# Two layers of sliding attention and SiLU feed-forward on one core: the planner's durations and DMA rings, and three moved steps

## The chip, the cores and the metric

The kernel runs on one core of a Trainium2 chip. The metric is its device time in microseconds (us). The core has five engines with a queue each, which run their instructions in order: TensorE (PE, matmuls; PEld is its weight load), VectorE (DVE), ScalarE (ACT), GpSimd (POOL) and SyncE (SP, which here only issues DMAs). An instruction starts when it is at the head of its queue and the semaphores that it waits for are there.

## The reference

The input has 2048 rows of 576 values. Two layers, each of two steps, with the same weights in both:

```python
x = x + _A_ref(_layernorm(x, axis=-1), A_wqkv, A_wo)
x = x + _B_ref(_layernorm(x, axis=-1), B_w1, B_w2)
```

`_A_ref` is attention with 32 heads of 18 values, where each row looks at 8 rows: itself and those 2, 4, ... 14 rows before it. `_B_ref` is a feed-forward: 576 to 4608 values, SiLU, and back to 576. All values are float32.

## The kernel before, in words

**Numbers.** Matmuls run in float16 with two halves for each operand: a high half and what is left of it. Three products (high by high, high by low, low by high) stand for one (`passes`). The scale of each weight is a power of two, found on the chip from the sum of its squares.

**Chunks and stages.** The rows are cut into four chunks of 512, each with four tiles of 128 rows (index `j`). A stage `s` from 0 to 7 is one chunk in one layer (`s = 4 * layer + chunk`). For each stage the work is: attention (`attention`, VectorE for the most part), its projection back into `x` (`project`), a layer norm, and a feed-forward (`ffn` for stages 0 to 2, `ffn_pairs` with fewer products for stages 3 to 7). "Chunk 1" and "second chunk" both mean stage 1. The q, k and v of chunks 1, 2 and 3 of the first layer are made early by `qkv_ahead`, while VectorE works on attention 0, and go through DRAM. Stage 0's feed-forward also splits the weights: raw tiles come by POOL's DMAs (L851 to L855), ScalarE sums their squares (L872, L874), PE adds them up over the partitions (L881, L882), ScalarE makes the high halves (L891, L896) and VectorE the low ones (L893, L898), and POOL stores them for the later stages. `prepare` then makes, for stages 3 to 7, the weights that `ffn_pairs` reads (`wfs`).

**Turning a tile.** `transposed` (L426) brings a tile of 128 rows with its 9 blocks of 128 columns into the form that PE needs. Either PE turns the nine blocks into PSUM (L435) and ScalarE copies them out (L437), or SP issues one DMA transpose (L439). `project` turns the attention tile `yh` into `yo` in the first way for stage 0, and by DMA for all others. Its matmuls are L817, 28 for each tile. The PSUM tiles `acc` (two, of two banks each) serve L435, L817 and the feed-forward's second product (L1157, L1096). Its first product is L1138 (`z`) or, in the pairs, L1042.

**Layer norm.** `layer_norm` has ways to get mean and variance: VectorE's `bn_stats` and `bn_aggr` (L481, L482), or, with `on_act == 2`, two passes of ScalarE with a sum (`total`: a copy, and a square of what is left when the mean is taken off), with VectorE's `mean` between them. The four norms that stand ahead of attention 0 use the first way.

**Scales of the feed-forward's middle.** `group_scale` (L907) makes, for a group of weights, a table of scales `sh` and its inverse `d2`, with four small VectorE instructions. After stage 0 it is called for four groups of nine weights (stages 1 and 2) and for four groups of 10, 8, 10 and 8 (the pairs).

**What sets the order.** The order of all instructions is made by a planner written into the kernel (`Plan`, L59). Each operation has an engine, a duration written into the code by hand, a priority (lower goes first), what it reads and writes, and `nbytes` if it is a DMA. `order` (L112) plays the program through: whenever an engine is free, the ready operation of the lowest priority whose buffers are free goes next. A DMA takes its issue time, then 1.2 us, its bytes at 0.33 MB per us (shared among the queues that have one under way), and 0.9 us; another engine sees an end 0.2 us later. The instructions are then written out in that order, each engine's queue in its own, and the chip runs them so whatever times come true. On the chip, DMAs of POOL on one hand, and those of SP and ACT on the other, take turns over eight semaphores; the order of `before` is made without them.

Of the kernel before, what the change touches and what calls it, by code (L numbers as in the profile page):

```python
# [16 lines left out]
P = 128  # L17
D = 576
# [36 lines left out]
class Op:  # L55
    __slots__ = ("eng", "dur", "fn", "prio", "seq", "deps", "outs", "n", "bufs", "nbytes", "start", "end", "table")


class Plan:  # L59
# [18 lines left out]
    def op(self, eng, dur, fn, reads=(), writes=(), prio=0.0, nbytes=0, table=None, after=()):  # L78
        o = Op()
        o.eng, o.dur, o.fn, o.prio, o.seq, o.nbytes, o.table = eng, dur, fn, prio, len(self.ops), nbytes, table  # L80
        o.outs, o.end = [], None
# [30 lines left out]
    def order(self):  # L112
# [10 lines left out]
        taken = {}  # L123

# [58 lines left out]
        while done < len(self.ops):  # L183
# [14 lines left out]
            for e in engines:  # L198
# [7 lines left out]
                while ready[e]:  # L206
                    x = heapq.heappop(ready[e])
                    need = [b for b in x[2].bufs if b.slot is None]
                    n = {}
                    for b in need:  # L210
                        n[b.tag] = n.get(b.tag, 0) + 1
                    if all(len(open_slots(t)) - want.get(t, 0) >= c for t, c in n.items()) and all(
                            self.turns[b.tag] in (None, b.turn) for b in need):
                        o = x[2]
                        break
                    for t, c in n.items():
                        want[t] = want.get(t, 0) + c
                    back.append(x)
# [22 lines left out]
                if o.nbytes:  # L241
                    queues[e].append([now + dur + self.DMA_IN, o.nbytes / self.DMA_RATE, o])
# [10 lines left out]
def sliding_attention_silu_ffn(ctx: ExitStack, tc: tile.TileContext, x, wqkv, wo, w1, w2, out):  # L253
# [143 lines left out]
    cg = cp.tile([P, NFT // G0], F32, name="cg")  # L397
    su = cp.tile([P, NU + 1], F32, name="su")
# [27 lines left out]
    def transposed(src, dst, key, j, prio, on_pe=False):  # L426


        if on_pe:
# [6 lines left out]
            op("PE", 0.8, turn, [(src, 0), (src, 1)], [m], prio)  # L436
            return op("ACT", 1.05, lambda: nc.scalar.activation(  # L437
                dst(), fl(T(m).bitcast(F16))[:, 0:9 * P].rearrange("p (a b) -> p a b", a=9), AF.Copy), [m], [(key, j)], prio - 9)
        return op("SP", 1.7, lambda: nc.sync.dma_start_transpose(dst(), fl(T(src))), [(src, 0), (src, 1)], [(key, j)], prio,  # L439
# [27 lines left out]
    def layer_norm(xs, prio, into, on_act, on_pe=False, late=[]):  # L467
# [18 lines left out]
        if on_act == 2:  # L486
            for j in range(NJ):
                op("ACT", 0.95, lambda j=j: total(j, 0), [xs[j]], [(st, j)], prio)
            op("DVE", 0.2, mean, [(st, j) for j in range(NJ)], [(nt, 0)], prio)
            for j in range(NJ):  # L490
                op("ACT", 0.95, lambda j=j: total(j, 1), [xs[j], (nt, 0)], [(st, j)], prio)
        else:
            for j in range(NJ):
                op("DVE", 1.15, lambda j=j: stats(j), [xs[j]], [(st, j), (mv, j)], prio)

        op("DVE", 2.4, lambda: newton(st, mv, nt, on_act, LNS), [(st, j) for j in range(NJ)] + [(mv, j) for j in range(NJ) if on_act != 2], [nt], prio)
        for j in range(NJ):
# [12 lines left out]
            if on_act in (1, 2) or on_act == 3 and j % 2 == 0:  # L510
                op("ACT", 0.74, lambda j=j, y=y: nc.scalar.activation(T(y), T(xs[j]), AF.Identity,
                                                                      bias=T(nt)[:, 2, j:j + 1]),
                   [xs[j], nt], [y, (xT, "hold")], prio)
                op("ACT", 0.74, lambda j=j, y=y, yh=yh: nc.scalar.activation(
                    fl(T(yh))[:, 0:D], T(y), AF.Copy, scale=T(nt)[:, 1, j:j + 1]), [y, nt], [(yh, 0)], prio)
                o = op("DVE", 0.95, lambda j=j, y=y, yh=yh: halves_lo(T(y), fl(T(yh)), T(nt)[:, 1, j:j + 1]),
                       [y, nt, (yh, 0)], [(yh, 1)], prio)
            else:
                op("DVE", 0.6, norm, [xs[j], (mv, j), nt] + late, [y, (xT, "hold")], prio)
                o = op("DVE", 1.2, halves, [y], [(yh, 0), (yh, 1)], prio)  # L520
# [20 lines left out]
    def raw_wq(u):  # L541
# [4 lines left out]
        for k in range(5):  # L546
# [8 lines left out]
            op("SP" if u else "ACT", 0.8 if k < 4 else 1.3, load, [], [rs[k]], WQ[u] if u else -20, nbytes=P * 3 * UC * 4, after=gate[3:4] if u > 1 else ())  # L555
            op("ACT", 0.8, square, [rs[k]], [("accq", u, k)], WQ[u])
# [10 lines left out]
        op("PE", 0.3, total, [("accq", u, k) for k in range(5)], [m], WQ[u])  # L567
        op("DVE", 0.9, scale, [m], [("su", u)], WQ[u])
        for k in range(5):
# [5 lines left out]
            op("ACT", 0.65, hi, [rs[k], ("su", u)], [w.keys[k]], WQ[u])  # L575
            op("DVE", 0.65, lo, [rs[k], ("su", u), w.keys[k]], [w.keys[5 + k]], WQ[u])
# [3 lines left out]
    def store_wq(u, w, m):  # L580
# [7 lines left out]
        op("POOL", 2.8 if w.kind == "h" else 0.6, store, w.keys, [("wqs", u)], -0.6, nbytes=P * 20 * QR, after=marks[m:m + 1])  # L588
# [10 lines left out]
    def raw_wo():  # L599
        rs = [Buf("w2") for _ in range(5)]  # L600
        p = -1.02
        for k in range(5):
# [9 lines left out]
            op("POOL", 0.6 if k < 4 else 1.2, load, [], [rs[k]], p, nbytes=P * D * 5,  # L612
               after=marks[PACE_WO[k]:PACE_WO[k] + 1])
            op("ACT", 0.9, square, [rs[k]], [("acco", k)], p)
# [10 lines left out]
        op("PE", 0.3, lambda: nc.tensor.matmul(T(m)[:, :5], ones, acco, start=True, stop=True),  # L625
           [("acco", k) for k in range(5)], [m], p)
        op("DVE", 1.6, scale, [m] + [("su", u) for u in range(NU)], ["so"], p)
        for k in range(5):
# [6 lines left out]
            op("ACT", 0.8, hi, [rs[k], "so"], [(WO, k)], p)  # L635
            op("DVE", 0.8, lo, [rs[k], "so", (WO, k)], [(WO, 5 + k)], p)
# [16 lines left out]
    def qkv_ahead(c, u, xT, w):  # L653
# [3 lines left out]
        for j in range(NJ):  # L657
            m, g = Buf("z"), Buf("w1" if c < 3 else "hs")
            op("PE", 2.6, lambda j=j, m=m: qkv_matmul(xT, w, j, m), [(xT, j)] + w.keys, [m], p)
            op("ACT", 0.65, lambda m=m, g=g: nc.scalar.activation(stage(g), T(m)[:, :QR], AF.Copy,  # L660
# [5 lines left out]
            op("SP", 0.9, store, [g], [("qd", c, u)], p, nbytes=P * QR * 4)  # L666

    def no_keys():
# [7 lines left out]
        op("POOL", 2.2, fn, [g], [("qd0", u) for u in range(NU)], -20, nbytes=50000)  # L676

    def attention(s, xT, wq, more=None):
# [4 lines left out]
        for u in range(NU):  # L683
            kv, qt = Buf("kv"), Buf("qt")
            own = [(kv, j) for j in range(NJ)]
            if wq is None:
                def fetch(kv=kv, qt=qt, u=u):
# [5 lines left out]
                op("SP" if s == 1 else "POOL", 1.2, fetch, [("qd", c, u), ("qd0", u) if blk == 0 else ("eds", lay, par, u)],  # L693
                   own + [(qt, j) for j in range(NJ)] + [(kv, "halo"), (kv, "edge")], pr_, nbytes=P * 4 * UC * 26)
            else:
                w = wq(u)
                if blk == 0:
# [3 lines left out]
                    op("POOL", 1.6, clear, [], [(kv, "edge")], pr_)  # L701
                else:
# [5 lines left out]
                    op("SP", 0.8, edge, [("eds", lay, par, u)], [(kv, "edge")], pr_, nbytes=20000)  # L708
                for j in range(NJ):
# [7 lines left out]
                    op("PE", 2.7 if s else 2.9, lambda j=j, m=m, w=w: qkv_matmul(xT, w, j, m),  # L717
                       [(xT, j)] + w.keys, [m, (kv, "hold")] if lay else [m], pr_)
                    op("ACT", 0.9, evac, [m, ("su", u)], [(kv, j), (qt, j)], pr_ - (0 if s else 9))
# [7 lines left out]
                op(*(("POOL", 2.6) if lay else ("ACT", 3.2)), halo, own, [(kv, "halo")], pr_ - 0.2, nbytes=P * 14 * UC * 4)  # L727
                if blk == 0:
# [7 lines left out]
                    op("POOL", 0.6, save, own, [("eds", lay, par, u)], pr_, nbytes=20000)  # L736
# [4 lines left out]
            for j in range(0, NJ, 2):  # L741
# [9 lines left out]
                op("DVE", 2.57, mul, keys + [(qt, j), (qt, j + 1)], [pr], pr_)  # L751
                op("DVE", 2.57, red, [pr], [(lg, j)], pr_)
# [14 lines left out]
            op("DVE", 1.25 if blk == 0 else 0.9, soft_a, [], lgs + [mx], pr_)  # L767
            op("ACT", 0.45, lambda pe=pe, lg=lg: nc.scalar.activation(T(pe), T(lg), AF.Exp, scale=DH ** -0.5),
               lgs, [pe], pr_ - 0.2, table="exp")
            op("DVE", 1.1, soft_b, [], [pe, sm], pr_)  # L770
            for j in range(0, NJ, 2):
                pr = Buf("pr")

                for a in range(2):
# [5 lines left out]
                    op("DVE", 1.33, mul, keys + [pe], [(pr, a)], pr_)  # L780
# [6 lines left out]
                op("DVE", 2.63, tree, [], [(pr, 0), (pr, 1), (o, j, u), (o, j + 1, u)], pr_)  # L787
                if s == 0:
                    marks.append(op("POOL", 0.2, lambda j=j, u=u: nc.gpsimd.tensor_copy(
# [3 lines left out]
    def project(s, o, xs):  # L793

        pr_ = s - 1.0
        for j in range(NJ):
# [12 lines left out]
            op(*(("ACT", 0.74) if s < 2 else ("DVE", 0.5)), hi, src, [(oh, 0)], pr_)  # L809
            op("DVE", 0.95, lo, src + [(oh, 0)], [(oh, 1)], pr_)  # L810
            transposed(oh, lambda oT=oT: T(oT), oT, j, pr_, s == 0)
# [7 lines left out]
            op("PE", 3.5, mm, [(oT, j)] + [(WO, k) for k in range(10)], [acc], pr_)  # L819
# [453 lines left out]
```

## Time and profile before

| | us |
|---|---|
| median of three timed runs | 2188.64 (2187.58 to 2190.4) |
| the profiled execution, its own time | 2198.78 |
| its span, first to last instruction | 2197.0 |
| granted TensorE clock over the span | 0.993 of full speed |

A profile shows one execution. Its groups give a line of the kernel, an engine, an operation and its tiles (written <- read, buffer numbers left out), how many there are, the busy time, the mean of one in ns, and the engine's idle time just before them with what ended it. A timeline row gives start, duration, engine, line, operation, tiles, count, and in brackets the idle time before it. A table by stretch gives the length of the stretch, the busy time and count of PE, PEld, DVE, ACT and POOL, and then the granted clock, the busy share of the DMA engines and GB/s.

### The profile page before, as it was taken

What the parts mean: (1) busy time and instruction counts of PE and PEld (TensorE: products, weight loads), DVE (VectorE), ACT (ScalarE), POOL (GpSimd) and SP (SyncE); (2) the same over time, 40 slices, a digit from 0 to 9 for tenths busy, and PEclk for the clock granted to TensorE, in tenths of its full rate; (3) what the DMA queues carried; (4) which work ended last, traced back from release to release, by engine and by line L of the source; (5) the groups of instructions that cost most, each with busy time, mean ns of one, the idle gap of its engine ahead of it and who ended that gap; (6) DMA issues with size and microseconds to landing.
All of it is one profiled execution on the core that took longest, in us unless ns stands there. A gap on an engine that the chain in (4) does not pass through costs nothing.

```text
span 2197.0 us, 40182 instructions
## 1 busy us (share of the span) xinstructions
PE 2132.9 (97%) x15784; PEld 1541.9 (70%) x15784; DVE 1598.0 (73%) x2513; ACT 927.2 (42%) x1697; POOL 380.9 (17%) x639
## 2 busy tenths in 40 slices
PE   5999999899999999999999999999999999999999
PEld 3555556566666666686788777887688867888887
DVE  7898888799999985456985489756995569753222
ACT  6445576544334444342343344253342424333232
POOL 2124355343133443101100010000000000000000
PEclk9999999999999999999999999999999999999999
DMA  5577567777687676686657765496565955566443
GB/s 154 159 204 258 175 224 228 197 223 241 184 223 253 234 216 202 211 232 179 180 143 184 208 209 175 127 240 160 176 187 136 250 153 162 156 174 183 141 146 108
DMA packets 318741, 417.23 MB, mean 190 GB/s; under 512 B 141640, under 2 KB 242612, under 8 KB 312280
## 3 DMA queue, kind: packets, MB, share of 16 engines
q1 hardware_dynamic: 279568, 280.31, 45.6%
q0 software_dynamic: 35712, 129.17, 18.3%
q10 hardware_dynamic: 3272, 5.19, 0.9%
q8 instruction: 123, 2.02, 0.4%
q14 instruction: 66, 0.54, 0.1%
HBM read 298.47 MB, written 67.68 MB: 167 GB/s over the span
## 4 chain that ended last, share of the span: by engine, by line
PE 87%; DMA 6%; DVE 4%; ACT 1%; issue 1%; POOL 0%; SPq 0%; ACTq 0%; DVEq 0%; POOLq 0%
PE acc L1096 24%; PE acc L1157 13%; PE z L1138 13%; PE z L1042 10%; PE misc L1042 10%; PE z L647 7%; PE misc L647 5%; PE acc L817 5%; DMA w<-wfs 2%; DMA yo<-yh 1%; DMA w<-in_B_w_dram 1%; DVE pr L778 1%; DMA h<-in_A_wqkv_dram 1%; DVE pr L785 1%; DVE yh L422 0%
## 5 line engine op out<-in xcount | busy, mean ns | idle before, releaser
L1096 PE MATMUL acc<-w,h 128*128 128x288 f16 x4320 | 549.3, 286 | 0.6 <-DVE x L1105 0.6
L1096 PEld LDWEIGHTS <-h 128*128 128x128 f16 x4320 | 422.7, 98 | 106.5 <-issue 0.8
L1042 PEld LDWEIGHTS <-w 128*128 128x128 f16 x4410 | 431.8, 98 | 67.9 <-DMA w<-wfs 8.2
L1138 PE MATMUL z<-xb,w 128*128 128x512 f16 x1512 | 336.9, 383 | 11.5 <-ACT hs L1140 4.2
L1157 PE MATMUL acc<-w,h 128*128 128x288 f16 x2592 | 321.7, 286 | 0.0
L1157 PEld LDWEIGHTS <-h 128*128 128x128 f16 x2592 | 253.7, 98 | 65.8
L1042 PE MATMUL misc<-xb,w 128*128 128x256 f16 x2226 | 280.3, 273 | 3.9 <-DVE wq L1049 2.2
L1138 PEld LDWEIGHTS <-w 128*128 128x128 f16 x1512 | 148.8, 99 | 191.0 <-DVE w L893 7.5
L1042 PE MATMUL z<-xb,w 128*128 128x256 f16 x2184 | 276.2, 273 | 5.6 <-DMA w<-wfs 4.0
L824 DVE SCALAR_TENSOR_TENSOR x<-acc,d,x 128x576 f32<-128x576 f32 x135 | 109.7, 813 | 189.7 <-PE acc L1096 152.8
L647 PEld LDWEIGHTS <-xa 128*128 128x128 f16 x1344 | 132.1, 99 | 118.3 <-issue 8.4
L745 DVE TENSOR_TENSOR pr<-qt,kv 128x2304 f32<-128x2304 f32 x64 | 163.4, 2553 | 20.7 <-DMA kv<-kv 19.5
L778 DVE TENSOR_TENSOR pr<-kv,pe 128x1152 f32<-128x1152 f32 x128 | 169.6, 1352 | 1.0
L749 DVE TENSOR_REDUCE lg<-pr 128x128 f32<-128x2304 f32 x64 | 163.1, 2549 | 1.4
L1140 ACT ACTIVATE hs<-z,d 128x512 f32<-128x512 f32 x108 | 73.7, 682 | 165.8 <-PE z L1138 162.3
L785 DVE TENSOR_TENSOR pr<-pr 128x1152 f32<-128x1152 f32 (+1 forms) x128 | 135.1, 1056 | 3.2
L817 PE MATMUL acc<-wo,yo 128*128 128x288 f16 x896 | 117.4, 290 | 9.7 <-DMA yo<-yh 8.0
L1075 DVE SCALAR_TENSOR_TENSOR h<-wq,sh,h 128x1024 f16<-128x1024 f32 x60 | 76.8, 1280 | 65.0 <-ACT h L1072 65.0
L647 PE MATMUL z<-wq,xa 128*128 128x432 f16 x602 | 116.6, 349 | 2.7 <-ACT w L660 2.0
L647 PE MATMUL misc<-wq,xa 128*128 128x432 f16 x574 | 112.0, 350 | 3.4 <-ACT xa L437 2.5
L817 PEld LDWEIGHTS <-yo 128*128 128x128 f16 x896 | 88.7, 99 | 35.2 <-DMA yo<-yh 8.8
L1145 DVE SCALAR_TENSOR_TENSOR h<-hs,sh,h 128x512 f16<-128x512 f32 x108 | 79.5, 746 | 34.7 <-ACT h L1142 34.4
(186 smaller groups left out, 2297.3 us busy)
## 6 DMA issues: line engine op xcount, KB each, us to landing
w<-wfs SPq DMA_DIRECT2D x630, 160.0 KB
w<-w2s SPq DMA_DIRECT2D x252, 288.0 KB
w<-w1s SPq DMA_DIRECT2D x72, 320.0 KB
wfs<-xa POOLq DMA_DIRECT2D x18, 1120.0 KB, 5.5
wq<-wqs SPq DMA_DIRECT2D x17, 1080.0 KB
kv<-kd POOLq DMA_DIRECT2D x8, 1584.0 KB, 8.6
w1s<-w POOLq DMA_DIRECT2D x36, 320.0 KB, 4.2
w<-in_B_w_dram POOLq DMA_DIRECT2D x36, 288.0 KB, 4.0
```

Of the source, the lines that this page charges most:

```text
L647: nc.tensor.matmul(T(m)[:, :3 * UC], a, b, start=n == 0, stop=n == len(pl) - 1)
L745: nc.vector.tensor_tensor(T(pr), T(qt)[:, j:j + 2, None, :].to_broadcast([P, 2, W, UC]), win(T(kv), j, 2), op=ALU.mult)
L749: nc.vector.tensor_reduce(T(lg)[:, j:j + 2].rearrange("p a w h -> p (a w h)"), T(pr).rearrange("p a w (h d) -> p (a w h) d", d=DH), axis=A ...
L778: nc.vector.tensor_tensor(T(pr)[:, a].rearrange("p w (h d) -> p w h d", d=DH), v, T(pe)[:, j + a, :, :, None].to_broadcast([P, W, UH, DH]) ...
L785: nc.vector.tensor_tensor(t[:, :, 0:h, :], t[:, :, 0:h, :], t[:, :, h:2 * h, :], op=ALU.add)
L817: nc.tensor.matmul(T(acc)[:, h, 0:288], a, b[:, h * 288:(h + 1) * 288], start=n == 0, stop=n == len(pl) - 1)
L824: nc.vector.scalar_tensor_tensor(t, T(acc)[:, :, 0:288], d, t, op0=ALU.mult, op1=ALU.add)
L1042: nc.tensor.matmul(t, w[:, u, :], v[:, r, :], start=first and m == 0, stop=m == 6, skip_group_check=True)
L1096: nc.tensor.matmul(T(acc)[:, h, 0:288], T(hb[t])[:, a, f, j * P:(j + 1) * P], T(wbs[t][f])[:, w, h * 288:(h + 1) * 288], start=t == 0 and ...
L1138: nc.tensor.matmul(T(z), v, u, start=m == 0, stop=m == len(pl) - 1)
L1145: op("DVE", 0.75, lambda hs=hs, h=h, f=f: nc.vector.scalar_tensor_tensor(T(h)[:, 1, :], T(hs), shs[i][:, f:f + 1], T(h)[:, 0, :], op0=ALU. ...
L1157: nc.tensor.matmul(T(acc)[:, h, 0:288], T(hb[q])[:, a, j * P:(j + 1) * P], T(wbs[q][0])[:, w, h * 288:(h + 1) * 288], start=q == 0 and m = ...
```

## The change

Four things.

1. **Durations.** Some seventy of the planner's durations are new. Most are smaller by 0.03 to 0.25 us: 0.82 to 0.75 (L891), 0.9 to 0.81 (L893), 0.7 to 0.61 (L1140), 0.85 to 0.75 (L824), 2.57 to 2.49 (L745, L749), 1.33 to 1.28 (L778), 1.15 to 0.99 (L481), 0.8 to 0.5 (L435), 1.7 to 1.34 (L439), 0.5 to 0.38 (SP's loads of weights). PE's barely move: 3.05 to 3.02 (L1138), 0.74 to 0.737 (L1096, L1157), 0.78 to 0.763 (L1042), 2.6 to 2.56 (L647), 3.5 to 3.43 (L817). Some grow: 1.1 to 1.38 (the second half of the softmax), 1.25 to 1.42 and 0.9 to 0.98 (its first half), 2.4 to 2.55 (`newton`), 6.0 to 7.2 (`prepare`'s load), 1.7 to 1.83 (L851), 0.2 to 1.3 (L789, POOL's pace mark).
2. **Rings.** Each DMA operation has a number of `lanes`, the DMAs that it issues. The planner keeps a ring of the DMAs issued by POOL, and one by SP and ACT together. An operation may go only when those that would be eight places back have landed.
3. **Moved steps.** The attention tiles of stage 1 are turned by PE (`s < 2` for `s == 0`), and the norm of chunk 3 ahead of attention 0 takes its statistics on ScalarE (`2` for `True`).
4. **Tables.** `tables` takes the place of the eight calls of `group_scale` after stage 0.

```diff
+        rings = {"POOL": [], "SP": []}
+        rings["ACT"] = rings["SP"]
+
+        def landed(o):
+
+            if not o.nbytes:
+                return True
+            r = rings[o.eng][-8:]
+            return len(r) + o.lanes <= 8 or all(d.end is not None and d.end <= now for d in r[:len(r) + o.lanes - 8])
...
-                    if all(len(open_slots(t)) - want.get(t, 0) >= c for t, c in n.items()) and all(
+                    if landed(x[2]) and all(len(open_slots(t)) - want.get(t, 0) >= c for t, c in n.items()) and all(
...
                 if o.nbytes:
+                    rings[e].extend([o] * min(o.lanes, 8))
...
-        op("POOL", 6.0, load, ["wsc"], [w], prio, nbytes=P * 12 * P * 4)
+        op("POOL", 7.2, load, ["wsc"], [w], prio, nbytes=P * 12 * P * 4, lanes=8)
...
-            transposed(oh, lambda oT=oT: T(oT), oT, j, pr_, s == 0)
+            transposed(oh, lambda oT=oT: T(oT), oT, j, pr_, s < 2)
...
+    def tables():
+
+        def fn():
+            both = s12.rearrange("p f i -> p i f")
+            n = 2 * (G2[0] + G2[1])
+            for i, m, cuts in ((1, G1, ((slice(0, 4), slice(0, G1)),)),
+                               (2, n, ((slice(0, 4, 2), slice(0, 2 * G2[0])), (slice(1, 4, 2), slice(2 * G2[0], n))))):
+                sh, d2 = shs[i], d2s[i]
+                nc.vector.scalar_tensor_tensor(sh, both[:, 0], HSH, both[:, 1], op0=ALU.mult, op1=ALU.mult)
+                v, r = (t.rearrange("p (g f) -> p g f", f=m) for t in (sh, r12.rearrange("p f i -> p i f")[:, 1]))
+                for g, f in cuts:
+                    nc.vector.tensor_reduce(cg4[:, g], v[:, :, f], axis=AX.X, op=ALU.min)
+                for g, f in cuts:
+                    w = f.stop - f.start
+                    nc.vector.tensor_tensor(v[:, :, f], r[:, :, f], cg4[:, g, None].to_broadcast([P, NFT // m, w]), op=ALU.mult)
+                nc.vector.reciprocal(d2, cg4)
+        op("DVE", 1.9, fn, [("s12", f) for f in range(NFT)], [("sh", i, g) for i in (1, 2) for g in range(4)] + ["cg4"], -0.5)
...
         if raw:
-            for g in range(NFT // G1):
-                group_scale(1, g, g * G1, (g + 1) * G1)
-            for g in range(len(G2)):
-                group_scale(2, g, 2 * sum(G2[:g]), 2 * sum(G2[:g + 1]))
+            tables()
             pair_scale()
...
-            x3 = layer_norm(load_x(3, -1.2, gate[11:12]), -1.2, "xa", True, PE_LN[3])
+            x3 = layer_norm(load_x(3, -1.2, gate[11:12]), -1.2, "xa", 2, PE_LN[3])
```

More of the change, by code (lines that the diff above doesn't have):

```diff
@@ L566, in scale @@
             nc.vector.tensor_scalar(du[:, u:u + 1], ru[:, u:u + 1], 1.0 / LNS, None, op0=ALU.mult)
-        op("PE", 0.3, total, [("accq", u, k) for k in range(5)], [m], WQ[u])
-        op("DVE", 0.9, scale, [m], [("su", u)], WQ[u])
+        op("PE", 0.2, total, [("accq", u, k) for k in range(5)], [m], WQ[u])
+        op("DVE", 0.75, scale, [m], [("su", u)], WQ[u])
         for k in range(5):
@@ L624, in scale @@
             nc.vector.tensor_scalar(DO, so[:, 3:4], ru[:, NU:], 1.0 / HSH, op0=ALU.mult, op1=ALU.mult)
-        op("PE", 0.3, lambda: nc.tensor.matmul(T(m)[:, :5], ones, acco, start=True, stop=True),
+        op("PE", 0.15, lambda: nc.tensor.matmul(T(m)[:, :5], ones, acco, start=True, stop=True),
            [("acco", k) for k in range(5)], [m], p)
-        op("DVE", 1.6, scale, [m] + [("su", u) for u in range(NU)], ["so"], p)
+        op("DVE", 1.1, scale, [m] + [("su", u) for u in range(NU)], ["so"], p)
         for k in range(5):
@@ L675, in fn @@
                 nc.gpsimd.dma_start(kd[1][u][0:W - 1, :], T(g)[0:W - 1, :2 * UC])
-        op("POOL", 2.2, fn, [g], [("qd0", u) for u in range(NU)], -20, nbytes=50000)
+        op("POOL", 2.2, fn, [g], [("qd0", u) for u in range(NU)], -20, nbytes=50000, lanes=4)
     def attention(s, xT, wq, more=None):
@@ L925, in fn @@
             nc.vector.tensor_scalar(dz, r12.rearrange("p (q f) i -> p q f i", f=2)[:, :, 0, 0], 2.0 / LNX, None, op0=ALU.mult)
[L926 removed]
+        op("DVE", 0.4, fn, [("s12", f) for f in range(NFT)], ["wsc"], -0.5)
     def prepare(q, prio):
```

188 lines of the change are left out of this document (94 added, 94 removed).

## The prediction

> **What bounds the kernel now.** I read the page first.
>
> ```profile
> span 2197.0 us, 40182 instructions
> PE 2132.9 (97%) x15784; PEld 1541.9 (70%) x15784; DVE 1598.0 (73%) x2513; ACT 927.2 (42%) x1697; POOL 380.9 (17%) x639
> ```
>
> TensorE (PE) is busy for 2132.9 of 2197.0 us. The change takes none of its matmuls away, so all that can be won is the 64.1 us in which PE isn't busy, and the time in which its clock is halved. Next, the busy times by stretch (PE, PEld, DVE, ACT, POOL, then the granted clock) say where these lie.
>
> ```profile
> 0.00:30.00 30.00, 8.33 (x46) 4.73 (x46) 16.82 (x64) 15.86 (x34) 8.91 (x19) 1.00 0.81 228
> 30.00:160.00 130.00, 125.12 (x731) 68.53 (x731) 119.02 (x211) 73.59 (x143) 26.49 (x32) 0.99 0.54 155
> 160.00:410.00 250.00, 234.37 (x1470) 142.21 (x1468) 219.79 (x357) 160.08 (x284) 117.92 (x203) 0.97 0.67 220
> 410.00:440.00 30.00, 22.22 (x151) 15.84 (x149) 18.26 (x30) 12.92 (x27) 8.44 (x15) 0.83 0.86 193
> 440.00:960.00 520.00, 519.74 (x3424) 334.79 (x3422) 427.93 (x626) 211.82 (x310) 161.04 (x271) 1.00 0.72 220
> 960.00:2197.00 1237.00, 1223.16 (x9974) 975.79 (x9971) 796.13 (x1229) 452.91 (x903) 58.08 (x100) 1.00 0.62 174
> ```
>
> Idle PE by subtraction: 21.7 us at the start, 4.9 to 160, 15.6 in 160:410, 7.8 in 410:440, 0.3 in 440:960 and 13.8 after that. So the kernel is three cases in one: a start that waits for its first loads, a first feed-forward (160 to 440, weights split on the fly) with 23.4 us of holes, and 1757 us that are all but full, where a new order can win little and lose much. Third, PE's waits in 160:410, its timeline around the hole of 410:440, and the slow stretches:
>
> ```profile
> PE z L1138 <- ACT hs L1140: 4.2, 2, 2.7
> PE z L1138 <- ACT w L891: 4.0, 2, 2.1
> ...
> PE z L647 <- ACT w L660: 2.0, 1, 2.0
> ```
> ```profile
> 200.48 0.67 PE L435 MATMUL acc<-ident,yh 128*128 128x128 f16 x9
> 200.99 2.72 PE L647 MATMUL z<-h,xa 128*128 128x432 f16 x14
> ...
> 365.39 0.39 PE L1138 MATMUL z<-xb,w 128*128 128x512 f16 x1 [1.84 <-ACT w L891]
> 366.68 4.60 PE L1138 MATMUL z<-xb,w 128*128 128x512 f16 x13 [0.90 <-DVE w L893]
> ...
> 422.22 2.37 PE L1157 MATMUL acc<-w,h 128*128 128x288 f16 x18
> 432.36 6.47 PE L817 MATMUL acc<-wo,yo 128*128 128x288 f16 x28 [7.78 <-DMA yo<-yh]
> 438.67 4.57 PE L1157 MATMUL acc<-w,h 128*128 128x288 f16 x36
> 443.08 3.59 PE L817 MATMUL acc<-wo,yo 128*128 128x288 f16 x28
> 452.51 3.19 PE L1138 MATMUL z<-xb,w 128*128 128x512 f16 x14
> ```
>
> The longest hole outside the start is 7.78 us at 432.36: the second chunk's projection (L817) waits for its attention tile to be turned by DMA. Then 28 matmuls take 6.47 us where the next 28 take 3.59: 2.88 us more are lost to the clock. The same shows at 366.68: 13 matmuls take 4.60 us after a hole of only 1.84 us, where 14 take 3.19 at 452.51, so about 1.7 us go after a short hole too.
>
> ```profile
> 166.00:172.00 6.00, 4.30 (x15) 1.94 (x15) 2.49 (x4) 1.80 (x4) 3.44 (x6) 0.72 0.61 187
> ...
> 364.00:370.00 6.00, 3.71 (x9) 1.29 (x10) 6.00 (x8) 5.68 (x11) 5.09 (x10) 0.72 1.00 312
> ```
>
> The first and the last of four such places in 160:410 stand here (the others lie at 248 and 286): a granted clock of 0.72 over 6 us, so 1.7 us lost at each, 6.8 in all. In that stretch 15.6 + 6.8 = 22.4 us could come back at most. The Trainium skill ("TensorE: Matmul & The Clock Gate", Part 1) has the clock fall to half after an idle window of about 3.4 us. Here a hole of 1.84 us was enough; by the page alone the short holes would cost no clock, and the 22.4 would be 15.6.
>
> **The change, part by part.** *Second chunk turned on PE.* L439's transposes of chunk 1 become nine PE transposes and a ScalarE copy per tile, as chunk 0 has them. Gone: 7.78 + 2.88 = 10.66 us. Added on PE: from 200.48 to the next start at 200.99, nine transposes take 0.51 us, four tiles 2.0 us. The copy is the row
>
> ```profile
> L437 ACT ACTIVATE yo<-acc 128x1152 f16<-128x1152 f16 x4 | 4.4, 1122 | 3.0 <-PE acc L435 3.0
> L435 PE MATMUL acc<-ident,yh 128*128 128x128 f16 x180 | 14.3, 228 | 8.5 <-ACT yh L514 3.4 <-DVE yh L508 2.9 <-DVE yh L422 2.2
> L853 POOL DMA_DIRECT2D w<-in_B_w_dram x72 | 38.4, 537 | 17.5 <-DMA w1s<-w 8.2 <-DMA w<-in_B_w_dram 4.0 <-DMA kv<-kd 2.0
> ```
> ```profile
> 193.61 7.03 PE L817 MATMUL acc<-wo,yo 128*128 128x288 f16 x56 [1.63 <-ACT yo L437]
> ```
>
> at 1.122 us each, 4.5 us for four; ScalarE is 43 to 64% busy around there, so it hides, but each copy stands in ScalarE's queue ahead of squares, splits and SiLUs of the feed-forward, and a PSUM bank pair (`acc`, two of them, shared with L1157) is held from turn to copy. In chunk 0 this cost one PE wait, 1.63 us. I take 2.0 + 1.6 = 3.6; the bounds are 2.0 and 8 (four such waits, 6.5, with 2.0 less what matmuls cover). SP loses four issues, which helps. Net: −10.7 + 3.6 = **−7.1 us**. The Trainium skill ("TensorE: Matmul & The Clock Gate", Part 4: PE-mode transpose) says that transposes don't count as work that keeps the clock up. In the trace the matmuls between the turns at 200 kept their pace (14 in 2.72 us), so I add nothing; if four turns ran together, one halved stretch of 1.7 us would make the net −5.4.
>
> *First statistics of chunk 3 on ScalarE.* Four times two `bn_stats` of 0.447 and an aggregate of 0.209 leave VectorE (DVE); eight ScalarE passes come, nearest rows 0.677 + 0.188:
>
> ```profile
> L481 DVE BATCH_NORM_STATS2 st<-x 128x6 f32<-128x288 f32 x88 | 35.7, 447 | 12.8 <-DMA x<-xd 6.9 <-DMA x<-in_A_x_dram 5.5
> L482 DVE BATCH_NORM_AGGREGATE mv<-st 128x2 f32<-128x12 f32 x44 | 9.2, 209 | 1.5
> L874 ACT ACTIVATE junk<-w 128x576 f16<-128x576 f32 x36 | 24.4, 677 | 11.1 <-DMA w<-in_B_w_dram 10.6
> L874 ACT ACTIVATION_READ_ACCUMULATOR junk<-w 128x1 f32 x36 | 6.8, 188 | 0.0
> L915 DVE TENSOR_SCALAR sh<-r,cg 128x6 f32<-128x6 f32 x6 | 1.4, 239 | 0.2
> ```
>
> DVE −4.4 us, ScalarE +6.9. This falls into 30:160, where DVE is busy 92% and ScalarE 57%: DVE brings attention 0 up to 4 us earlier. But PE has only 4.9 us of holes there, and work of other chunks, so I count 0 (bounds −2 and +2; the new wait is DVE's short mean between the two ScalarE passes, and behind it stands attention 0's work, which has other operations to run).
>
> *Scale tables.* Eight groups of four small DVE instructions (about 0.16 to 0.24 us each, 32 in all) become ten in one operation: about 3 us of DVE saved. All of it now waits for the last weight's scale; but the last splits' own matmuls then still lie ahead on PE, so nothing waits: 0.
>
> *Durations and rings.* This moves every instruction. Nearly all durations shrink by 0.05 to 0.1 us to the step between starts in the trace; GpSimd's grow where they were short. DMA issues now keep a place in rings of eight. The trace bears that out: L853 sat 8.2 us behind the landing of an older store, a wait that the old plan doesn't know. So the plan of the first feed-forward was made against DMAs that ran late, and PE's holes there (ScalarE and DVE weight splits that came late) are what a truer plan can close. It can't close all: PE is 94% and DVE 88% busy in 160:410, and some holes are true shortage of split weights. Bounds: −22.4 (all) and +5. I take **−8**, two of the four places with their clock (such as 1.84 + 0.90 + 1.7 and 2.7 + 1.7). In 440:960 there is 0.3 us to win, so a new order can only lose: I take **+1**, bound +18 (the rival below). After 960:
>
> ```profile
> PE z L1042 <- DMA w<-wfs: 4.0, 3, 2.8
> ```
>
> The 13.8 us of 960:2197 are such small waits and a tail; a new order wins or loses among them: 0, bounds −6 and +8.
>
> **The sum.** −7.1 − 8 + 1 = −14 us against the profiled run of 2198.78 us (span 2197.0, and 1.8 around it): 2184.7. The median of the three timed runs, 2188.64, is 10.1 us below the profiled run; I carry that over: **2174.6**, I say 2175.
>
> **The rivals.** *A. The truer plan closes most holes of the first feed-forward:* −7.1 − 20 − 3 after 960 gives 2158.6. For it: in 440:960, with no raw weights to split, the planner left 0.3 us idle. Against: DVE at 88% in 160:410.
>
> *B. The new waits eat the gain,* so that the change doesn't do what it is to: the turns wait for banks and for ScalarE (8 for 3.6), the rest of the first feed-forward stays as it is, and 2 to 4 us of new holes come elsewhere: −10.7 + 8 + 3 = 0, so 2188. For it: ScalarE's in-order queue at 400 is full of splits. Against: chunk 0 does the same for 1.63 us.
>
> *C. Slower: the third chunk's projection, still turned by DMA, becomes the hole.* The chain of waits has these two pieces:
>
> ```profile
> 415.06 17.25 DMA yo<-yh
> ...
> 596.73 12.14 DMA yo<-yh
> ```
> ```profile
> 605.47 3.19 PE L1138 MATMUL z<-xb,w 128*128 128x512 f16 x14
> 608.91 3.60 PE L817 MATMUL acc<-wo,yo 128*128 128x288 f16 x28 [0.26 <-DMA yo<-yh]
> ```
>
> The transfer at 596.73 took 12.14 us and cost PE only 0.26, because the old plan, with DVE's durations too long, had other matmuls there. The planner's own figure for such a transfer is issue 1.34 + start 1.2 + 0.59 MB at 0.33 MB per us, 1.79, + end 0.9 = 5.2 us on a quiet queue. With exact durations PE comes to L817 by that figure, and waits 12.14 − 5.2 = 6.9 us and 1.7 to 2.9 for the clock, twice for chunk 2 (its second and third tile): 17 to 20. With the first feed-forward unchanged that is −7.1 + 17.5 = +10.4: 2199. It decides the sign from 7.1 us of such holes on. For it: DMA was 86% busy in 410:440 where the transfer took 17.25, and the ring rule doesn't slow a transfer. Against: the rule delays issues in the plan, loads are fewer in chunk 2, and no later chunk shows such a wait beside the 0.3 us of 440:960.
>
> **How the numbers follow.** Forecast (2166 to 2184) 0.46; A (2150 to 2166) 0.18; B (2184 to 2193) 0.17; C (2193 to 2206) 0.19. A measurement of this kernel tells about 0.2% (4.4 us) from no change, so faster means below 2184.3: 0.46 + 0.18 = 0.64; same, 2184.3 to 2193.0: 0.17; slower: 0.19. The range 2157 to 2198 leaves out the outer half of A and of C, some 0.2 in all.
>
> **What would show it.** Right: no PE wait of L817 for `DMA yo<-yh` between 400 and 460, L435 with 216 transposes, clock 1.00 there; 160:410 with about half its holes and two places at 0.72; 440:960 still under 2 us idle. Wrong: PE waits for `ACT yo L437` beyond 3 us in all (B), an L817 wait at chunk 2 beyond 5 us (C), or more idle after 960 than 22 us, which no step above has. It would also be wrong if PE's holes before 440 keep their size under other names: then DVE or the raw loads set them, and no plan does.

## The result and the profile after

| | before | changed |
|---|---|---|
| median of 22 timed runs each, us | 2188.35 | 2184.97 |
| lowest and highest, us | 2179.99 to 2196.03 | 2178.64 to 2190.95 |
| profiled execution, its own time, us | 2198.78 | 2180.11 |
| its span, us, and granted clock | 2197.0, 0.993 | 2178.3, 0.998 |

The ratio of the times is 0.9983, 95% interval 0.9972 to 0.9995: 3.4 us faster, where 13.6 were forecast. By the bound of 0.2% named in the prediction it counts as the same. The two profiled executions are 18.7 us apart, five times as far as the medians. Both differences need an explanation.

The busy times by stretch of the changed kernel, columns as in the prediction (the stretch 160:440 is taken as one; before had 234.37 + 22.22 = 256.59 us of PE there):

```profile
0.00:30.00 30.00, 8.52 (x37) 4.46 (x38) 16.59 (x63) 15.39 (x33) 8.90 (x19) 1.00 0.80 228
30.00:160.00 130.00, 126.80 (x756) 70.06 (x754) 118.40 (x201) 80.10 (x160) 26.06 (x32) 1.00 0.56 157
160.00:440.00 280.00, 270.34 (x1800) 172.02 (x1799) 262.96 (x427) 189.98 (x332) 128.24 (x221) 0.99 0.67 222
440.00:960.00 520.00, 514.83 (x3399) 332.68 (x3398) 404.81 (x592) 206.74 (x306) 158.34 (x267) 1.00 0.72 223
960.00:2200.00 1240.00, 1205.38 (x9838) 961.61 (x9835) 782.99 (x1200) 439.82 (x887) 57.87 (x100) 1.00 0.61 170
```

Idle PE in 160:440 fell from 23.4 to 9.7 us, and its clock rose from 0.97 and 0.83 to 0.99. In 440:960 it rose from 0.3 to 5.2 us. PE's timeline shows the second chunk's projection (now L828) and what the prediction's rival C spoke of, one chunk later:

```profile
386.71 1.17 PE L446 MATMUL acc<-ident,yh 128*128 128x128 f16 x18
387.71 3.29 PE L1167 MATMUL z<-xb,w 128*128 128x512 f16 x14
...
391.21 7.02 PE L828 MATMUL acc<-wo,yo 128*128 128x288 f16 x56
398.06 6.21 PE L1167 MATMUL z<-xb,w 128*128 128x512 f16 x28
...
404.47 1.17 PE L446 MATMUL acc<-ident,yh 128*128 128x128 f16 x18
405.47 3.19 PE L1167 MATMUL z<-xb,w 128*128 128x512 f16 x14
408.49 7.02 PE L828 MATMUL acc<-wo,yo 128*128 128x288 f16 x56
```
```profile
740.77 4.93 PE L828 MATMUL acc<-wo,yo 128*128 128x288 f16 x28 [3.33 <-DMA yo<-yh]
745.54 2.37 PE L1186 MATMUL acc<-w,h 128*128 128x288 f16 x18
```

The turns of chunk 1 stand in pairs (18 transposes in 1.00 us from start to next start), other matmuls fill the time of the copy, and L828 has no bracket: it waits for nothing. At 740.77 chunk 3's projection, still turned by DMA, waits 3.33 us, and its 28 matmuls take 4.93 us against 3.59.

### The profile page after: what moved, and what is told of

It is laid out like the page before. It is cut to its first block, busy times and chain, and to the rows that moved or that the text cites. A ratio compares the mean times of both kernels' runs of the same rounds, so it can differ in the third digit from the quotient of the medians.

```text
span 2178.3 us, 40221 instructions
## 1 busy us (share of the span) xinstructions
PE 2125.9 (98%) x15820; PEld 1540.8 (71%) x15820; DVE 1585.8 (73%) x2479; ACT 932.0 (43%) x1715; POOL 379.4 (17%) x639
## 4 chain that ended last, share of the span: by engine, by line
PE 71%; DVE 15%; DMA 7%; issue 3%; POOL 1%; ACT 1%; ACTq 0%; SPq 0%; DVEq 0%; POOLq 0%
PE acc L1125 23%; PE z L1071 10%; PE misc L1071 10%; PE acc L1186 7%; PE z L1167 6%; PE z L658 6%; PE misc L658 5%; PE acc L828 4%; DVE pr L789 2%; DVE lg L760 2%; DMA w<-wfs 2%; DVE pr L796 2%; DVE pr L756 2%; DMA wq<-in_B_w_dram 1%; DVE xa L992 1%
## 5 line engine op out<-in xcount | busy, mean ns | idle before, releaser
L1167 PE MATMUL z<-xb,w 128*128 128x512 f16 x1512 | 331.8, 379 | 6.4 <-ACT w L902 2.0
L1186 PE MATMUL acc<-w,h 128*128 128x288 f16 x2592 | 321.9, 286 | 0.0
L1186 PEld LDWEIGHTS <-h 128*128 128x128 f16 x2592 | 253.7, 98 | 65.7
L1071 PE MATMUL z<-xb,w 128*128 128x256 f16 x2240 | 281.9, 273 | 2.5 <-DMA w<-wfs 1.3
L1071 PE MATMUL misc<-xb,w 128*128 128x256 f16 x2170 | 273.4, 273 | 5.5 <-DMA w<-wfs 4.5
L658 PEld LDWEIGHTS <-xa 128*128 128x128 f16 x1344 | 132.3, 99 | 119.6 <-issue 10.1
L789 DVE TENSOR_TENSOR pr<-kv,pe 128x1152 f32<-128x1152 f32 x128 | 169.7, 1352 | 1.1
L828 PE MATMUL acc<-wo,yo 128*128 128x288 f16 x896 | 115.7, 288 | 3.3 <-DMA yo<-yh 3.3
L1075 ACT ACTIVATE wq<-misc 128x256 f32<-128x256 f32 x85 | 32.0, 376 | 187.0 <-PE misc L1071 187.0
```

Source lines behind the costliest of these rows:

```text
L658: nc.tensor.matmul(T(m)[:, :3 * UC], a, b, start=n == 0, stop=n == len(pl) - 1)
L789: nc.vector.tensor_tensor(T(pr)[:, a].rearrange("p w (h d) -> p w h d", d=DH), v, T(pe)[:, j + a, :, :, None].to_broadcast([P, W, UH, DH]) ...
L828: nc.tensor.matmul(T(acc)[:, h, 0:288], a, b[:, h * 288:(h + 1) * 288], start=n == 0, stop=n == len(pl) - 1)
L1071: nc.tensor.matmul(t, w[:, u, :], v[:, r, :], start=first and m == 0, stop=m == 6, skip_group_check=True)
L1167: nc.tensor.matmul(T(z), v, u, start=m == 0, stop=m == len(pl) - 1)
L1186: nc.tensor.matmul(T(acc)[:, h, 0:288], T(hb[q])[:, a, j * P:(j + 1) * P], T(wbs[q][0])[:, w, h * 288:(h + 1) * 288], start=q == 0 and m = ...
```

## The experiments

Theories were set against each other as they came up. First: the first profile of before caught an odd execution (theory 1), or the gain is real and given back elsewhere (2). Then: the clock makes the spread (A) or a rare transfer does (B). Last: the ring rule made the plan better (theory C, which isn't the prediction's rival C), the gain went to the remaining DMA transposes (E), or every edit just draws a new plan (D): a new order of the same work, good or bad by chance. Times are medians, the ratio is to before, timed beside it on the same chip.

### Before, profiled twice more

No edit. Expected:

> The kernel before, unchanged, profiled once more. Theory 1 (the first profile caught an odd execution: one transfer of 17.25 us, which made most of the 10.1 us between that execution and the median): PE's wait of L817 at chunk 1 is under 3 us, the span 2180 to 2190, the granted clock above 0.994. Theory 2 (the hole of 10.7 us is in every execution and the changed kernel gives the gain back elsewhere): the wait at L817 of chunk 1 is again 6 to 9 us with a halved clock behind it.

> The kernel before, a third profile, for the spread from execution to execution. Theory 1: the wait at chunk 1 is again under 3 us, and other holes (160 to 410 us) differ by less than 3 us in sum between the profiles. Theory 2: 6 to 9 us again.

Spans 2187.9 and 2187.4 us, 9 us below the first profile's 2197.0, both with a clock of 0.995 against 0.993. PE's timeline around chunk 1's projection, from the second profile and then from the third, which has one earlier row too:

```profile
425.11 5.27 PE L817 MATMUL acc<-wo,yo 128*128 128x288 f16 x28 [6.59 <-DMA yo<-yh]
430.21 4.57 PE L1157 MATMUL acc<-w,h 128*128 128x288 f16 x36
```
```profile
285.67 3.18 PE L1138 MATMUL z<-xb,w 128*128 128x512 f16 x14 [2.82 <-ACT hs L1140]
...
426.27 6.00 PE L817 MATMUL acc<-wo,yo 128*128 128x288 f16 x28 [5.65 <-DMA yo<-yh]
```

The hole is there each time (6.59, 5.65, first 7.78): theory 1 falls in its strong form, though its span and clock came true. The first profile was an odd one, by holes that are a little longer and a clock that was halved more often. The row at 285.67 shows how: after 2.82 us of idleness 14 matmuls ran at full pace in 3.18 us. In the first profile the same place, after a hole of 2.67 us, has

```profile
288.01 4.87 PE L1138 MATMUL z<-xb,w 128*128 128x512 f16 x14 [2.67 <-ACT hs L1140]
```

The same program, the same wait, and 1.7 us more in one execution than in the next. The stretches from 160 us on, in the second profile of before:

```profile
160.00:440.00 280.00, 259.60 (x1675) 162.55 (x1674) 243.70 (x397) 174.47 (x313) 128.98 (x220) 0.97 0.69 219
440.00:960.00 520.00, 519.48 (x3429) 335.03 (x3427) 423.56 (x619) 214.95 (x315) 158.96 (x268) 1.00 0.73 223
960.00:2200.00 1240.00, 1214.46 (x9900) 968.55 (x9897) 792.54 (x1224) 447.19 (x893) 57.88 (x100) 1.00 0.62 171
```

### The turn alone, and all but the turn

```diff
-            transposed(oh, lambda oT=oT: T(oT), oT, j, pr_, s == 0)
+            transposed(oh, lambda oT=oT: T(oT), oT, j, pr_, s < 2)
```

The first is before with this edit, the second the changed kernel with it undone.

> The kernel before with one edit: the attention tiles of chunk 1 are turned by PE. Its time against before gives the turn's worth under the old durations. Theory 1: within 3 us of before either way (2.0 us of transposes more, against a hole that is mostly not there). Theory 2: 5 to 9 us faster than before.

> The changed kernel without the turn (chunk 1 goes by DMA again), all other parts kept. Theory 1: within 3 us of the changed kernel, so 2182 to 2188. Theory 2: 5 to 9 us slower than the changed kernel, 2190 to 2194, with a PE wait of 5 us or more for a DMA transpose at chunk 1.

The turn alone: 2195.99, ratio 1.0038 (1.0026 to 1.0050), slower, which neither theory had. All but the turn: 2191.91, ratio 1.0018 (1.0007 to 1.0030), slower too, and in theory 2's range. Together they are 0.9983. The parts don't add. In the first, chunk 1's hole is gone and others have come, on PE's timeline (this execution, 2191.45, is the fastest of its twelve):

```profile
455.54 0.39 PE L1138 MATMUL z<-xb,w 128*128 128x512 f16 x1 [2.49 <-ACT w L891]
456.93 8.97 PE L1138 MATMUL z<-xb,w 128*128 128x512 f16 x27 [1.00 <-DVE w L893]
...
485.84 4.65 PE L1138 MATMUL z<-xb,w 128*128 128x512 f16 x13 [2.31 <-DMA xb<-yh]
```

The layer norm's DMA transpose (`xb<-yh`) now ends late where the projection's did. In the second, PE's waits of 440:960 are

```profile
PE acc L828 <- DVE x L835: 2.6, 2, 1.4
PE acc L828 <- DMA yo<-yh: 2.5, 1, 2.5
PE acc L1125 <- DVE h L1104: 1.3, 2, 0.7
```

and the wait of 5 us or more that theory 2 expected at chunk 1 isn't there:

```profile
389.52 3.60 PE L828 MATMUL acc<-wo,yo 128*128 128x288 f16 x28 [0.21 <-DMA yo<-yh]
394.86 3.60 PE L828 MATMUL acc<-wo,yo 128*128 128x288 f16 x28 [1.74 <-DMA yo<-yh]
```

With the other parts of the change, chunk 1's tiles go by DMA as in before and cost PE 1.95 us in all, and no clock (28 matmuls in 3.60 us). The turn is one way to close that hole; the rest of the change, in this plan, all but closes it too.

### The changed kernel, profiled again

> The changed kernel, unchanged, profiled a second time. Theory A (holes of the same size halve the clock in one execution and not in the next, and the first profile of the changed kernel, with two halved stretches, was a lucky one): span 2181 to 2187, four or more stretches of halved clock, PE idle time within 3 us of the first profile's 48.8. Theory B (an occasional long DMA, as at the third layer's chunk 3, makes the spread): the clock as before, and one hole of 4 us or more that the first profile lacks.

Span 2183.7 us, clock 0.996; the first profile had 2178.3 and 0.998.

```profile
160.00:440.00 280.00, 271.09 (x1807) 172.70 (x1806) 264.45 (x437) 191.22 (x334) 129.63 (x223) 0.99 0.67 224
440.00:960.00 520.00, 513.72 (x3383) 331.88 (x3382) 402.38 (x580) 204.51 (x302) 157.65 (x265) 0.99 0.73 221
960.00:2200.00 1240.00, 1209.40 (x9845) 963.53 (x9843) 783.81 (x1203) 441.08 (x888) 57.99 (x100) 1.00 0.61 170
```
```profile
740.18 6.39 PE L828 MATMUL acc<-wo,yo 128*128 128x288 f16 x28 [4.09 <-DMA yo<-yh]
```

PE's 15820 instructions are busy for 2129.2 us, in the first profile for 2125.9: 3.3 of the 5.4 us between the two are the same matmuls at a lower clock, and 2.1 are idle time (52.4 to 54.5 us; the expectation's 48.8 is not the first profile's figure). In steps of 5 us, the granted clock is under 0.9 at five places, in the first profile at three. That is theory A for the most part. Chunk 3's hole is again there, a little longer (4.09 us, and 28 matmuls in 6.39).

### Without the ring rule

```diff
-                    if landed(x[2]) and all(len(open_slots(t)) ...
+                    if all(len(open_slots(t)) ...
```

> The changed kernel, but the planner asks no longer whether the DMAs eight places back have landed; durations, turn, tables and statistics as changed. Theory C (the ring rule is what makes the plan of the first feed-forward truer): 3 to 8 us slower than the changed kernel, with PE's holes between 160 and 410 us back at 13 to 16 us. Theory D (each plan is a new draw, and no part has a worth of its own): anywhere within 8 us of the changed kernel, with holes in other places rather than more holes in 160 to 410.

2179.13, ratio 0.9958 (0.9942 to 0.9974): faster than the changed kernel, against theory C. Idle PE is 8.1 us in 160:440 and 2.1 in 440:960:

```profile
160.00:440.00 280.00, 271.94 (x1810) 173.09 (x1809) 262.44 (x436) 192.52 (x335) 129.52 (x221) 0.99 0.68 225
440.00:960.00 520.00, 517.90 (x3444) 336.96 (x3443) 414.81 (x601) 209.20 (x311) 158.56 (x267) 1.00 0.72 227
```

### The two steps costed at nothing, alone

```diff
-            x3 = layer_norm(..., "xa", True, PE_LN[3])
+            x3 = layer_norm(..., "xa", 2, PE_LN[3])
...
-            for g in range(NFT // G1): group_scale(1, ...)
-            for g in range(len(G2)): group_scale(2, ...)
+            tables()
```

> The kernel before with the two steps that were costed at nothing: the tables made at once and chunk 3's first statistics on ScalarE; old durations, no rings, no turn. If their direct cost is nothing and the plan keeps its shape: within 2 us of before, and the hole at chunk 1 stays at 5 to 8 us. Theory D: up to 8 us off either way, with the holes moved.

2201.97, ratio 1.0049 (1.0033 to 1.0065), some 11 us slower, which is beyond both expectations. Their own instructions don't cost that: against the first profile of before, VectorE is busy 6.5 us less (1591.5 us) and ScalarE 1.0 us more (928.2). The plan changed around them, and PE's waits of 160:440 grew:

```profile
PE acc L818 <- DMA yo<-yh: 11.5, 2, 5.8
PE z L1157 <- ACT hs L1159: 5.6, 2, 3.4
PE z L1157 <- ACT w L892: 3.4, 2, 2.0
PE acc L818 <- ACT yo L438: 3.1, 1, 3.1
```

### Chunks 2 and 3 turned by PE too, with and without rings

```diff
-            transposed(oh, lambda oT=oT: T(oT), oT, j, pr_, s < 2)
+            transposed(oh, lambda oT=oT: T(oT), oT, j, pr_, s < 4)
```

The second has the ring rule taken out as well.

> The changed kernel with the attention tiles of chunks 2 and 3 turned by PE too, so that no projection of the first layer waits for a DMA transpose. Eight tiles more cost 4.1 us of PE; the hole at chunk 3 (3.3 us and 1.3 of clock in the first profile) goes. Theory E (the change's gain is given back at the DMA transposes that are left): the same or up to 2 us faster than the changed kernel. Theory D: anywhere, 2 us slower in the mean for the added work.

> The changed kernel without the ring rule and with chunks 2 and 3 turned by PE too: the two variants that came out faster, together. If both had a worth of their own: about 0.9958 x 0.9964 / 0.9983 = 0.994 of before, near 2176. If each is a draw of the plan (theory D): between 0.994 and 1.000, and no better than the variant without rings alone.

2181.30, ratio 0.9964 (0.9952 to 0.9976), and 2180.43, ratio 0.9963 (0.9946 to 0.9979). Both are faster than before, and the hole at chunk 3 is gone. In the first, 440:960 has 1.6 us of idle PE and its full clock; in the second, PE's waits there are one row:

```profile
440.00:960.00 520.00, 518.40 (x3491) 338.51 (x3491) 402.34 (x580) 211.92 (x312) 156.29 (x264) 1.00 0.67 217
```
```profile
PE z L1167 <- ACT hs L1169: 1.0, 1, 1.0
```

But the two gains don't add (0.994 was expected of that), and the first, 3.7 us below the changed kernel, is more than theory E's 2 us. E explains the direction of the first, D allows both.

### The new durations alone

Before with all new durations, and nothing else of the change.

> The kernel before with the new durations and nothing else (no rings, no turn, old tables, old statistics). If the truer durations are what clears the holes of 160 to 440 us: idle time plus clock loss there falls from 28 to 15 us or less even without the turn, and the time is 3 us or more under before. If the moved steps or the turn are needed for it: over 20 us there, and no gain.

2197.13, ratio 1.0041 (1.0023 to 1.0058), slower, although 160:440 is much fuller than before's:

```profile
160.00:440.00 280.00, 268.77 (x1772) 170.07 (x1770) 267.02 (x439) 182.46 (x322) 128.18 (x224) 1.00 0.71 230
440.00:960.00 520.00, 509.77 (x3357) 328.38 (x3356) 402.26 (x600) 207.91 (x307) 156.78 (x264) 0.99 0.71 222
```
```profile
477.61 4.81 PE L1167 MATMUL z<-xb,w 128*128 128x512 f16 x11 [7.71 <-DMA xb<-yh]
```

The idle 11.2 us of 160:440 confirm the first half of the expectation; the gain of 3 us or more that goes with it didn't come. What was won there is lost at 477.61, at a layer norm's DMA transpose. That is so for this execution, whose 2188.17 us are the fastest of eleven and no slower than before; where the other 9 us up to the median go, the profile can't show.

### Eight edits that mean nothing

Each changes one number that only the planner reads:

```diff
-    LAT = 0.2
+    LAT = 0.21
```
```diff
-                op("PE", 3.02, mm, ...
+                op("PE", 3.03, mm, ...
```

(3.05 to 3.06 in before). The operations stay the same, and only their order can differ.

> The changed kernel with one number of the planner changed that means nothing on the chip: 0.21 for 0.2 us from an end to what waits for it. The operations are the same; only their order can differ. Theory D (a new draw alone moves the time by several us): 3 us or more off the changed kernel, either way, with other holes. Otherwise: within 1.5 us of it.

> A second number that means nothing on the chip: 3.03 for 3.02 us for the first product's matmuls in the planner, all else as changed. Theory D: again 3 us or more off the changed kernel, and not by the same amount as the other. Otherwise: within 1.5 us of it.

> The kernel before with 0.21 for 0.2 us in the planner, nothing else. If before is an ordinary draw of its plan: within 10 us of it, either way. If before was a lucky draw (its order was kept because it ran well), this is slower by 4 us or more, as the re-drawn variants of the changed kernel were by 8 and 16.

> The kernel before with 3.06 for 3.05 us for the first product's matmuls in the planner, nothing else. The same two cases as for the other null edit of before; together they give the middle of the old plan's draws.

> The changed kernel without the ring rule, and 0.21 for 0.2 us in the planner. If the ring rule itself costs time: again near 2179, 10 us or more below the same null edit with rings (2200.7). If the variant without rings was a lucky draw: 2188 to 2200.

> The changed kernel without the ring rule, and 3.03 for 3.02 us in the planner. If the ring rule itself costs time: near 2179, 10 us or more below the same null edit with rings (2193.2). If draws alone: 2185 to 2200.

> The changed kernel with chunks 2 and 3 turned by PE too (2181.3), with 0.21 for 0.2 us in the planner. If turning all the first layer's projections on PE has a worth of its own: 5 us or more below the changed kernel with the same null edit (2200.7), and no wait for a DMA transpose between 440 and 960 us. If it was a lucky draw: 2193 to 2203.

> The same kernel with 3.03 for 3.02 us for the first product's matmuls in the planner. A worth of its own: 5 us or more below the changed kernel with the same null edit (2193.2). A lucky draw: 2190 to 2200.

| plan | as it stands | latency 0.21 | matmul + 0.01 |
|---|---|---|---|
| before | 2188.35 | 2194.86, 1.0026 (1.0008 to 1.0045) | 2197.61, 1.0038 (1.0014 to 1.0062) |
| changed | 2184.97 | 2200.70, 1.0067 (1.0045 to 1.0090) | 2193.20, 1.0029 (1.0014 to 1.0044) |
| changed, no rings | 2179.13 | 2192.10, 1.0023 (1.0005 to 1.0040) | 2194.28, 1.0033 (1.0016 to 1.0051) |
| changed, turned to chunk 3 | 2181.30 | 2203.95, 1.0067 (1.0045 to 1.0088) | 2199.08, 1.0048 (1.0033 to 1.0062) |

All eight are slower than before, by 4 to 16 us; their mean is 2197.0. The two of before lie at 2196.2 in the mean, the two of the changed kernel at 2197.0. Each plan is 6.5 to 22.7 us better as it stands than with a null edit, and the places among the plans don't hold: with the same null edit the kernel without rings is once 8.6 us below the changed kernel and once 1.1 above it, and the one turned to chunk 3 is above it both times (3.3 and 5.9 us). So before and the changed kernel both look like lucky draws, and no worth of rings or of more turns is shown. PE's timeline of the changed kernel with 3.03:

```profile
413.90 0.39 PE L892 MATMUL misc<-accw,ones 128*128 128x4 f32 x2 [3.14 <-ACT junk L885]
...
416.44 0.61 PE L1167 MATMUL z<-xb,w 128*128 128x512 f16 x1 [1.86 <-ACT w L902]
419.78 4.45 PE L1167 MATMUL z<-xb,w 128*128 128x512 f16 x10 [2.73 <-DVE w L904]
```

The last raw weights come late, and three holes of 7.7 us with a halved clock stand where the changed kernel has none.

But these are not independent draws, for all six null edits of the changed kernel and its two variants lose in this stretch. In 160:440 they have 19 to 22 us of idle PE; the seven profiles of plans with the new durations as they stand (the changed kernel twice, its variants without the turn, without rings, with chunk 3 turned and with both of these, and the durations alone) have 8 to 11. POOL's queue shows the same split. First two rows of the changed kernel, then two with 3.03:

```profile
413.88 0.77 POOL L862 DMA_DIRECT2D w<-in_B_w_dram  x1
430.14 0.54 POOL L866 DMA_DIRECT2D w<-in_B_w_dram  x1 [13.21 <-PE acc L1186]
```
```profile
407.38 0.55 POOL L866 DMA_DIRECT2D w<-in_B_w_dram  x1 [16.34 <-PE acc L1186]
443.62 0.78 POOL L862 DMA_DIRECT2D w<-in_B_w_dram  x1
```

Both times a load (L866) at the head of POOL's queue waits until PE's second product (L1186) is done with its buffer. In the changed kernel all loads of L862 are out by then; with 3.03 the later ones stand behind it, and the last goes 30 us later. In the seven profiles the last L862 goes between 410 and 414 us, in the six between 439 and 451. That this order makes the holes is read off the timelines; no run moves it alone. The null edits of before leave 160:440 as it was (19.1 and 19.0 us idle) and lose behind it (3.0 and 4.6 us idle in 440:960, before 0.3 to 0.6).

And before with 3.06 has rival C at the place and tile for which it was written, chunk 2:

```profile
599.97 5.26 PE L817 MATMUL acc<-wo,yo 128*128 128x288 f16 x28 [3.34 <-DMA yo<-yh]
605.06 1.24 PE L1138 MATMUL z<-xb,w 128*128 128x512 f16 x5
```

## Why the prediction was right up to 440 us and wrong behind it

A sum from typical to typical shows where the forecast of −14 us missed. It takes the mean of before's second and third profile (the third had 259.28, 519.42 and 1216.06 us of PE in the last three stretches) against the second profile of the changed kernel; their spans differ by −4.0 us, the medians by −3.4. Clock loss is PE's busy time times what the granted clock lacks of 1, added up in steps of 2 us. All in us:

| stretch | forecast | idle PE | clock loss | added transposes | sum |
|---|---|---|---|---|---|
| up to 160 | 0 | −0.9 | −0.9 | | −1.7 |
| 160:440 | −7.1 − 8 = −15.1 | 20.6 to 8.9, −11.7 | 6.0 to 1.6, −4.4 | +2.0 | −14.0 |
| 440:960 | +1 | 0.6 to 6.3, +5.7 | 0 to 2.9, +2.9 | | +8.6 |
| after 960 | 0 | 12.4 to 14.3, +1.9 | 1.6 to 2.8, +1.2 | | +3.1 |
| all | −14.1 | | | | −4.0 |

**440:960: the step that failed.** "In 440:960 there is 0.3 us to win, so a new order can only lose: I take +1". It lost 8.6 us (5.9 in the first profile of the changed kernel), and with it went the prediction's own sign, "440:960 still under 2 us idle". The mechanism is rival C's, at chunk 3 in place of chunk 2. Chunk 3's projection waits 3.33 and 4.09 us for its DMA transpose, and its 28 matmuls take 1.3 and 2.8 us more than 3.59: 4.7 and 6.9 us of the 5.9 and 8.6. With chunk 3 turned by PE too, 1.6 us idle and a full clock are left there, so +1 would have been about right for that plan. In the plan without rings chunk 3 goes by DMA and that hole doesn't come (2.1 us idle): whether such a transpose comes late is a matter of the order too. I gave C its price only for chunk 2 and for the sign; the milder form, one hole of 3 to 4 us at any chunk still turned by DMA, belonged into the forecast.

**After 960: 0 was too low as well.** It was +3.1 here, inside the bounds of −6 and +8; in the first profile of the changed kernel it was about −1, so this part is mostly a matter of the execution.

**The base of the sum was a risk that did no harm.** "The median of the three timed runs, 2188.64, is 10.1 us below the profiled run; I carry that over". The profiled execution was indeed odd: 9 us longer than two more profiles, with 4 to 5 us more idle PE and 4 to 5 us more of busy PE for the same matmuls (2132.9 against 2128.0 and 2128.5). In 160:440 alone it had 2.8 us more idle and 3.5 us more clock loss than the mean of the other two. A saving that takes all these holes off and then moves down to the median would count them twice. But the sum took 15.1 of some 33 us there (23.4 idle, 9.5 of clock), and the typical execution still had that much to give. Only chunk 1's hole was taken at its odd size, 10.66 us; the other two profiles have 8.27 and 8.06.

**Chunk 1's turn: right in the place, and its worth isn't the turn's alone.** The hole is in all three profiles of before and in neither of the changed kernel. It was taken 2.5 us too large, and the wait of 1.6 us for the copy didn't come; the two errors nearly cancel. But without the turn the rest of the change leaves only 1.95 us of the hole, and the durations alone leave 0.64 us of it. By itself the turn makes the kernel slower, 1.0038.

**The first feed-forward: right in size, for a reason that doesn't hold.** The stretch gave 14.0 of the 15.1 us. The reason given was that a truer plan closes the holes. The new durations by themselves do bring 160:440 to 11.2 us idle; but 0.01 us more in one of the changed kernel's, no less true, brings 18.7 us back (280 less 261.26). So the gain hangs on the order that came out, and that it came out as forecast is luck. One reading was off too: the slow 13 matmuls at 366.68 follow not one hole of 1.84 us but two, 1.84 and 0.90, with one matmul between them.

**Durations and rings as a term.** I priced a new order by what it could mend. Its spread was the thing to price: null edits move a plan by 6.5 to 22.7 us, where the whole forecast is 13.6. With that the chance of "faster" should have been well under 0.64, because the kernel before is better than both of its null edits.

**Open:** whether the change is worth anything on average over orders. Two null edits each, 2.8 us apart for before and 7.5 for the changed kernel, can't show a difference of 3 us. Which of the planner's choices a null edit tips was not followed up, nor whether other numbers in the code had been fitted to 0.2 and to the durations as they stand, which would also make every null edit slower.

## What to carry to other kernels

Where an edit closes a wait in a stretch that was full behind it, price the like places too: here the hole at chunk 1's DMA transpose went and one at chunk 3's came, so its price belongs into the forecast and not only into a rival. Where a planner orders a kernel that is 97% busy on one engine, change a planner number that means nothing, a few times, and take that spread as the unit in which any edit of the plan is judged; then look by stretch at what the null edits have in common, for here six of them lost at one place. Compare the profiled execution with the median before taking anything off it, and compare term by term with a second profile: a hole of an odd execution is larger than the median's.

## What the runs showed of the hardware that was not expected

Whether a hole of two to three us halves the clock is a matter of the execution, not of the hole's length alone. At one place in one program 14 matmuls took 4.87 us after 2.67 us of idleness in one execution, and 3.18 us after 2.82 us in another; after the 5.65 to 7.78 us at chunk 1 the 28 matmuls took 5.27 to 6.47 us each time, against 3.59 at full pace. Such places move this kernel by 3 to 5 us from run to run (PE busy 2128.0 to 2132.9 us in before, clock 0.995 to 0.993; 2125.9 to 2129.2 us in the changed kernel, clock 0.998 to 0.996). It fits what the Trainium skill says of the clock gate ("TensorE: Matmul & The Clock Gate", Part 1), that the window it watches runs freely; that the two are the same thing is argued, not shown.
